# Zero products in three waits of the head, and seven unread transfers taken out

## The chip, the cores and the metric

The kernel runs on one core of a Trainium2 chip. The metric is the device time of one execution in microseconds (us); the time of a kernel is the median of its runs.

## The reference

Two stages, for 4 batches of 12,544 rows of 128 numbers. The first is attention through 32 inducing vectors, the second a maxout layer with two weight matrices:

```python
def mab(q, kv):
    s = scale * (q @ kv.transpose(0, 2, 1))
    s = s - s.max(-1, keepdims=True)
    a = np.exp(s)
    a /= a.sum(-1, keepdims=True) + 1e-09
    return a @ kv
h = mab(I, x)          # I: inducing, 32 x 128, for each of 4 batches
attn = mab(x, h)       # 4 x 12544 x 128
...
h1 = x @ w1            # x: attn as 50176 x 128; w1, w2: 128 x 1024
h2 = x @ w2
g = np.maximum(h1, h2)
return (g @ w_out)     # w_out: 1024 x 128
```

## The kernel before, in words

The maxout is rewritten: max(h1, h2) = h1 + relu(h2 - h1). With w21 = w2 - w1, the first part needs only w1 @ w_out (the tile w1out), and the second a ReLU over the product with w21. As the attention's output is a weighted mean of the 32 rows of h, the product h @ w21 (the tile hwd) is formed once for each batch, and each chunk of 128 rows of x needs only its weights over the 32 rows (the tile e2, exponentials that are divided by their sum at the end).

All engines' orders are written out by hand. The kernel is straight-line code made by a Python program that carries a planner's clock along (class Clock, the object `ck`): `ck.pe`, `ck.act`, `ck.dve`, `ck.pool` and `ck.sp` are the times at which it thinks each engine is free, `ck.bank[i]` the time at which PSUM bank i is free again. `bank()` hands out the bank that comes free first; it marks nothing by itself. `ck.wait(t, why)` moves the planner's PE to t if t is later, `ck.run(us)` adds work to it and a turn between product shapes (`mode`). Real waits are made by semaphores, whatever the planner thinks.

The **head** (batch 0, from L826 on). Nine products of a tile of zeros (`warm`, L831 and L832) run first. x comes in twelve parts. `HEAD` (L858) is a string of words: `1a`, `1b` turn the two halves of a part with PE and copy them out with VectorE and ScalarE (`p1_transpose`, L304); `I` turns the inducing vectors (`head_ind`, L836), whose result `inducingT` VectorE writes at L840; `S0` and so on are a part's scores (`p1_scores`, L323, products at L328); `A0` and so on sum the parts up (`p1_accum`, L352, products at L365 and L374). Then come the small steps: h, its sums (`small_sums`, L543), the first two pieces of hwd (`small_hwd`, L554, product at L569, eviction at L573), the first chunk's exponentials, and one more `fill`, which is so many products of the zeros (L821).

The **stream** follows the string `ORDER` (L1171). `s` is a chunk's exponentials; `p4.9` is a phase (L1099) of up to four units of 32-row products side by side, L1154, each of which a ReLU eviction follows (`relu_out`, L1083: L1091 on VectorE or L1094 on ScalarE, as the bits of the second number say); a bare number is so many products with w_out at L979. The first words are `s p4.9 s p2.2 H1 V W p2.2`. `H1` is the third piece of hwd (step 2 of `small_hwd`: 512 columns, evicted by VectorE), which waits for the last difference w21 that POOL forms at L616. `V` (`weights_2`, L628) turns w1: eight transposes at L634, the second four after POOL's cast at L625; VectorE copies the first four out at L639 and ScalarE the others at L642. `W` (`weights_3`, L647) multiplies that with w_out, eight products at L651, which wait for both copies.

On **SP's queue** the head issues two loads of x and one of the inducing vectors (L277, L278). L291 then issues seven transfers inside the on-chip memory, of 8, 12, 14, 15, 4, 2 and 1 partitions and 16 to 28 bytes each, from the first loaded part of x to a corner of a ReLU buffer (`probe`); nothing reads what they write. They wait for that part. After them SP carries the transposing transfers (L241) and the stores of the output (L1039). The other loads are issued from POOL.

Of the kernel before, what the change touches and what calls it, by code (L numbers as in the profile page):

```python
# [16 lines left out]
INF = 1e9  # L17
# [140 lines left out]
def kernel(  # L158
# [9 lines left out]
    nc = tc.nc  # L168
# [24 lines left out]
    ck = Clock()  # L193
    uid = [0]
    psall = psum.tile([128, 8, 512], F32, name="psall", tag="psall")
    relus = [big.tile([128, 2, 4096], F16, name=f"relus{q}", tag=f"relus{q}") for q in range(4)]
# [3 lines left out]
    def bank(shape, dtype=F32, only=None):  # L200
        i = min(range(8), key=lambda j: ck.bank[j]) if only is None else only
        ps = psall[:, i, :]
        if dtype == F16:
            ps = ps.bitcast(F16)
            if len(shape) == 3:
                ps = ps.rearrange("p (k c) -> p k c", c=128)
            ps = ps[:, 0 : shape[1]]
        return i, ps
# [8 lines left out]
    xn_at = {}  # L217
# [36 lines left out]
    warm = consts.tile([128, 512], F16, name="warm")  # L254
# [7 lines left out]
    w1T = w1s[:, J : 2 * J].rearrange("p (j c) -> p j c", c=C)  # L262
    w21 = consts.tile([C, J], F16, name="w21")
# [2 lines left out]
    inducingT = consts.tile([C, M], F16, name="inducingT")  # L266
    m1bd = consts.tile([128, 4, C], F16, name="m1bd")
    repd = consts.tile([128, 128], F32, name="repd")
    probe = relus[2][0:16, 1, 3968:4096]
    pace = consts.tile([128, 1], F32, name="pace")  # L270

    with tc.manual_schedule(engines={ET.PE, ET.DVE, ET.Activation, ET.Pool, ET.SP}):
# [14 lines left out]
            nc.gpsimd.dma_start(out=w1f[:, sl], in_=moe_w1[:, sl])  # L287
            nc.gpsimd.dma_start(out=w2f[:, sl], in_=moe_w2[:, sl])
        nc.gpsimd.dma_start(out=woutp, in_=moe_w_out.rearrange("(jb j) c -> j jb c", j=128))
        for i, k in enumerate((8, 12, 14, 15, 4, 2, 1)):  # L290
            nc.sync.dma_start(out=probe[0:k, 16 * i : 16 * i + 8 + i], in_=xn_at[0, 1][0:k, 0, 0 : 8 + i])  # L291
        nc.vector.memset(warm, 0.0)
        nc.vector.memset(ones16, 1.0)
        nc.vector.memset(minus1, -1.0)
# [259 lines left out]
        def small_hwd(b, steps=(0, 1), vector=True):  # L554

            if b == 0:
                cuts = ((0, 256), (256, 512), (512, 1024))
            else:
                cuts = ((0, 512), (512, 1024))
            if 0 in steps:  # L560
                st[b]["hwd"] = smp.tile([128, J], F16, name=f"hwd_{b}", tag="hwd")
            hwd = st[b]["hwd"]
            for step in steps:
                lo, hi = cuts[step]
                w, sl = hi - lo, slice(lo, hi)
                bi, ps = bank([128, 512])
                ps = ps[:, 0:w]
                ck.wait(max(ck.bank[bi], st[b]["hT4r"], w_of.get(("w21", lo), 0.0) if b == 0 else 0.0), "p1")
                nc.tensor.matmul(out=ps, lhsT=st[b]["hT4"], rhs=w21[:, sl], start=True, stop=True)  # L569
                end = ck.run(0.215 * w / 512)  # L570
                if b == 0:
                    if vector:
                        nc.vector.tensor_scalar(  # L573
                            out=hwd[:, sl],
                            in0=ps,
                            scalar1=st[0]["rs"],
                            scalar2=1.0 / scale,
                            op0=ALU.mult,
                            op1=ALU.mult,
                        )  # L580
                    else:
                        nc.scalar.activation(out=hwd[:, sl], in_=ps, func=AF.Copy, scale=st[0]["rw"])
                elif step == 0:
                    nc.vector.tensor_copy(out=hwd[:, sl], in_=ps)
                else:
                    nc.scalar.copy(out=hwd[:, sl], in_=ps)
                if vector if b == 0 else step == 0:
                    ck.bank[bi] = ck.on_dve(end, 0.07 + w / 970.0)
                else:
                    ck.bank[bi] = ck.on_act(end, 0.06 + w / 1200.0)  # L590
                for piece in range(lo // 256, hi // 256):
                    st[b]["hw", piece] = ck.bank[bi]
# [19 lines left out]

        w_of = {}

        def difference(eng, lo, hi, ready, us):
            eng.tensor_sub(w21[:, lo:hi], w2f[:, lo:hi], w1f[:, lo:hi])  # L616
            w_of["w21", lo] = ck.on_dve(ready, us) if eng is nc.vector else ck.on_pool(ready, us)

        def cast_w1(h):
            sl = slice(512 * h, 512 * (h + 1))  # L620
            if h == 0:
                nc.vector.tensor_copy(out=w1h[:, sl], in_=w1f[:, sl])
                ck.on_dve(20.4, 0.33)
            else:
                nc.gpsimd.tensor_copy(out=w1h[:, sl], in_=w1f[:, sl])  # L625
                w_of["cast"] = ck.on_pool(0.0, 0.8)
# [19 lines left out]

        def weights_3():  # L647
            bi, ps = bank([128, 512])
            ck.wait(max(ck.bank[bi], w_of["w1T"]), "w")
            for jb in range(NJB):  # L650
                nc.tensor.matmul(  # L651
                    out=ps[:, 0:128],
                    lhsT=w1T[:, jb, :],
                    rhs=woutp[:, jb, :],
                    start=(jb == 0),
                    stop=(jb == NJB - 1),
                )
            end = ck.run(0.056 * NJB)
            nc.scalar.copy(out=w1out, in_=ps[:, 0:128])
            ck.bank[bi] = w_of["w1out"] = ck.on_act(end, 0.2)  # L660
# [158 lines left out]
            ck.bank[bi] = ck.on_dve(end, 0.18 + 0.001 * 4 * n)  # L819

        def fill(n):  # L821
            bi, ps = bank([128, 512])
            for _ in range(n):
                nc.tensor.matmul(out=ps, lhsT=warm[:, 0:128], rhs=warm, start=True, stop=True)
            ck.run(0.22 * n)


        nc.vector.tensor_copy(out=xn_at[0, 0][:, 0:8, :], in_=xf[:, 0:8, :])  # L828
# [1 line left out]
        bi, ps = bank([128, 512])  # L830
# [25 lines left out]
        ck.pe, ck.act = 7.18, 6.25  # L856
        p1_transpose(0, 0, 1)
        HEAD = """  # L858
        1a 1b I S0 2a 2b S1 A0 S2 3a 3b A1 4a 4b S3 S4 A2 A3 5a 5b A4 6a 6b S5 7a 7b S6 A5 8a 8b S7
        A6 9a 9b 10a S8 11a N S9 S10 A7 S11 A8 A9 A10 A11  # L860
        """
        for word in HEAD.split():
            if word == "I":
                head_ind()
            elif word == "N":
                cast_w1(0)
            elif word[0] == "S":
                p1_scores(0, int(word[1:]))
            elif word[0] == "A":
                p1_accum(0, int(word[1:]))  # L870
            else:
                p1_transpose(0, int(word[:-1]), "ab".index(word[-1]))
# [207 lines left out]
            jobs = sorted(jobs, key=lambda e: e[0])[:n]  # L1080
            return gl, [e[1:] for e in sorted(jobs, key=lambda e: e[1])]

        def relu_out(q, blk, unit, bi, ready, vector):  # L1083

            _, t0, w, u = unit
            jpb, w4 = 4 // w, blk.quarters[q].w
            dst = blk.relu[q][:, 0 : NJB * w4 * 128].rearrange("p (j t) -> p j t", j=NJB)
            dst = dst[:, u * jpb : (u + 1) * jpb, 128 * t0 : 128 * (t0 + w)]
            src = psall[:, bi, :].rearrange("p (j t) -> p j t", j=jpb)
            if vector:  # L1090
                nc.vector.tensor_scalar(out=dst, in0=src, scalar1=0.0, scalar2=None, op0=ALU.max)  # L1091
                t = ck.on_dve(ready, 0.604)
            else:
                nc.scalar.activation(out=dst, in_=src, func=AF.Relu)  # L1094
                t = ck.on_act(ready, 0.484)
            ck.bank[bi] = t
            blk.done[q, t0, u] = t

        def phase(n, vector=0):  # L1099
            gl, jobs = pick(n)  # L1100
            free = sorted(range(8), key=lambda j: ck.bank[j])[: len(jobs)]
            got = []
            for (q, blk, unit), bi in zip(jobs, free):
                _, t0, w, u = unit
                pieces = range(u * (4 // w) // 2, ((u + 1) * (4 // w) - 1) // 2 + 1)
                staged = blk.first if blk.first is not None and t0 + w <= 2 else blk.staged
                ready = max([ck.bank[bi], staged] + [st[blk.b]["hw", p] for p in pieces])
# [8 lines left out]
            if gl is not None:  # L1116
                q, b = gl.q, gl.blk.b
# [3 lines left out]
                        out=gl.ps[:, 128 * s : 128 * (s + 1)],  # L1121
                        lhsT=gl.blk.e2[r, 128 * t : 128 * (t + 1)],
# [8 lines left out]
            for q, blk, (_, t0, w, u), bi, ps, ready in got:  # L1131
                r = slice(32 * q, 32 * (q + 1))
                jpb = 4 // w
# [30 lines left out]
            for k, (q, blk, unit, bi, _, _) in enumerate(got):  # L1164
                ready = ends[k] + 0.025
                ptr[q][1] += 1
                state["issued"] += 1
                relu_out(q, blk, unit, bi, ready, bool(vector >> k & 1))

        state["stage"] = 1  # L1170
        ORDER = """  # L1171
# [43 lines left out]
            "p": phase,  # L1215
        }
        for word in ORDER.split():
            if word == "s":
                stage(blocks[state["stage"]])
                state["stage"] += 1  # L1220
            elif word.isdigit() or word[0] == "n":
                narrow = word[0] == "n"
                for _ in range(int(word.lstrip("n"))):
                    ready = final_ready()
                    if not narrow:
                        keep_busy(ready)
                    ck.wait(ready, "relu")
                    final_one(narrow)
            else:
                WORK[word[0]](*[int(n) for n in word[1:].split(".") if n])  # L1230
# [32 lines left out]
```

## Time and profile before

| | us |
|---|---|
| median of 3 runs | 315.84 (315.37, 315.84, 316.93) |
| the profiled execution | 315.13 |
| its span in the trace | 313.3 |
| PE busy in the span | 306.2 (98%) |
| ScalarE (ACT) busy | 280.9 (90%) |
| VectorE (DVE) busy | 273.4 (87%) |
| GpSimd (POOL) busy | 122.4 (39%) |

PE is the matmul engine, PEld its loading of weights, DVE is VectorE, ACT ScalarE, SP the engine whose queue issues most transfers; L569 is line 569 of the kernel. A row of the timeline gives start, length (both us), engine, line and operation, output and inputs, the shapes (for products: rows by columns of the weights, then the moving operand), how many in a row, and in brackets the idle time ahead of them with what ended it. A row of the chain in order of time gives start, length and what the time went to. A row of the waits gives who waited for whom, the total in us, how often, and the longest. Products are pipelined: the length of a row holds the tail of its last product, so the distance between starts says what a product costs.

### The profile page before, as it was taken

What the parts mean: (1) busy time and instruction counts of PE and PEld (TensorE: products, weight loads), DVE (VectorE), ACT (ScalarE), POOL (GpSimd) and SP (SyncE); (2) the same over time, 40 slices, a digit from 0 to 9 for tenths busy, and PEclk for the clock granted to TensorE, in tenths of its full rate; (3) what the DMA queues carried; (4) which work ended last, traced back from release to release, by engine and by line L of the source; (5) the groups of instructions that cost most, each with busy time, mean ns of one, the idle gap of its engine ahead of it and who ended that gap; (6) DMA issues with size and microseconds to landing.
All of it is one profiled execution on the core that took longest, in us unless ns stands there. A gap on an engine that the chain in (4) does not pass through costs nothing.

```text
span 313.3 us, 12580 instructions
## 1 busy us (share of the span) xinstructions
PE 306.2 (98%) x5310; PEld 239.7 (76%) x5310; DVE 273.4 (87%) x485; ACT 280.9 (90%) x581; POOL 122.4 (39%) x183
## 2 busy tenths in 40 slices
PE   8998999999999999999999999999999999999996
PEld 3875777777877777778877887778778877788885
DVE  2468999998889999989899999999999899989894
ACT  3768999999989989999999999989999899998875
POOL 7364008900530006567600563238205742388000
PEclk9999999999999999999999999999999999999999
DMA  7999988999499999997899899993422522352223
GB/s 203 209 260 205 215 223 187 155 235 226 112 205 245 253 208 198 204 185 196 190 239 258 180 228 204 215 200 130 133 86 103 153 101 89 117 130 104 103 88 135
DMA packets 80931, 55.69 MB, mean 178 GB/s; under 512 B 62410, under 2 KB 65770, under 8 KB 80874
## 3 DMA queue, kind: packets, MB, share of 16 engines
q1 hardware_dynamic: 74906, 41.19, 56.7%
q0 software_dynamic: 5968, 13.70, 22.6%
q8 instruction: 41, 0.67, 0.9%
q14 instruction: 16, 0.13, 0.1%
HBM read 27.28 MB, written 25.69 MB: 169 GB/s over the span
## 4 chain that ended last, share of the span: by engine, by line
PE 89%; DMA 6%; ACT 2%; DVE 1%; SPq 1%; issue 1%; POOL 0%; POOLq 0%
PE psall L979 58%; PE psall L1154 21%; DMA xn<-in_x_dram 2%; PE psall L701 2%; DMA xT<-xn 2%; DMA eT<-eu 2%; PE psall L312 1%; PE psall L461 1%; PE psall L402 1%; ACT relus L1094 1%; PE psall L374 1%; PE psall L328 1%; SPq L241 1%; DVE relus L1091 1%; PE psall L569 1%
## 5 line engine op out<-in xcount | busy, mean ns | idle before, releaser
L1094 ACT ACTIVATE relus<-psall 128x512 f16<-128x512 f32 x468 | 239.2, 619 | 15.9 <-PE psall L1154 14.8
L1091 DVE TENSOR_SCALAR relus<-psall 128x512 f16<-128x512 f32 x308 | 195.5, 683 | 16.7 <-PE psall L1154 15.8
L979 PE MATMUL psall<-woutp,relus 128*128 128x128 f16 x3104 | 203.9, 220 | 0.0
L979 PEld LDWEIGHTS <-relus 128*128 128x128 f16 x3104 | 174.9, 98 | 33.5 <-issue 27.7
L1154 PE MATMUL psall<-e,hwd 32*128 32x512 f16 (+2 forms) x840 | 81.1, 362 | 0.0
L765 POOL TENSOR_TENSOR half<-ed 128x256 f32<-128x256 f16 (+2 forms) x22 | 13.4, 611 | 147.0 <-DMA ed<-e 147.0
L769 POOL TENSOR_TENSOR rd<-den,minus 128x16 f32<-128x16 f32 (+2 forms) x22 | 57.8, 2628 | 1.7
L1014 DVE TENSOR_TENSOR osbs<-psall,rd 128x512 f32<-128x512 f32 (+1 forms) x80 | 50.9, 637 | 4.6 <-PE psall L1154 1.6
L1154 PEld LDWEIGHTS <-hwd 32*128 32x128 f16 x880 | 27.8, 91 | 11.6 <-issue 2.3
L1154 PE MATMUL psall<-m,e 32*128 32x128 f16 x372 | 36.6, 216 | 0.0
L1154 PEld LDWEIGHTS <-e 32*128 32x128 f16 x372 | 22.2, 92 | 9.7 <-issue 2.0
L765 POOL TENSOR_TENSOR half<-half 128x32 f32<-128x32 f32 (+4 forms) x66 | 21.4, 324 | 5.2
L228 POOL DMA_DIRECT2D xn<-in_x_dram x32 | 17.6, 562 | 5.6 <-DMA xn<-in_x_dram 4.3
L1014 DVE TENSOR_TENSOR osbs<-psall,rp 128x512 f32<-128x512 f32 (+3 forms) x24 | 15.6, 649 | 0.5 <-PE psall L1154 0.4
L316 DVE COPY xT<-psall 128x512 f16<-128x512 f16 (+3 forms) x12 | 5.7, 485 | 8.5 <-PE psall L312 8.5
L416 ACT ACTIVATE eu<-psall 128x512 f16<-128x512 f32 x18 | 10.8, 611 | 0.3 <-PE psall L402 0.2
L714 ACT ACTIVATE e<-psall 128x512 f16<-128x512 f32 (+2 forms) x21 | 10.9, 574 | 0.1
L319 ACT COPY xT<-psall 128x768 f16<-128x768 f16 (+3 forms) x10 | 5.8, 575 | 4.6 <-PE psall L312 4.5
L701 PE MATMUL psall<-xT,hT 128*32 128x512 f16 (+3 forms) x110 | 8.4, 362 | 0.0
L312 PE MATMUL psall<-identity,xn 128*128 128x128 f16 x98 | 8.0, 229 | 0.4 <-DMA xn<-in_x_dram 0.3
L312 PEld LDWEIGHTS <-xn 128*128 128x128 f16 x98 | 6.1, 103 | 2.3 <-DVE xn L828 1.0
L402 PE MATMUL psall<-xT,inducingT 128*32 128x512 f16 x72 | 6.3, 381 | 0.0
(114 smaller groups left out, 128.2 us busy)
## 6 DMA issues: line engine op xcount, KB each, us to landing
out_dram<-osbs SPq DMA_DIRECT2D x90, 256.0 KB, 2.5
xn<-in_x_dram POOLq DMA_DIRECT2D x24, 448.0 KB, 9.6
out_dram<-osbs SPq DMA_DIRECT2D x10, 128.0 KB, 5.8
relus<-in_moe_w_dram POOLq DMA_DIRECT2D x4, 256.0 KB, 5.8
xn<-in_x_dram POOLq DMA_DIRECT2D x4, 224.0 KB, 10.3
xT<-xn SPq DMA_TRANSPOSE x33, 4.1
relus<-in_x_dram SPq DMA_DIRECT2D x1, 512.0 KB
relus<-in_x_dram SPq DMA_DIRECT2D x1, 384.0 KB
```

The lines of the kernel that those rows point to most:

```text
L228: nc.gpsimd.dma_start(out=xn_at[b, i][:, 0:n, :], in_=xr[b, :, k0 : k0 + n, :])
L312: nc.tensor.transpose(ps[:, j, :], xn[:, g + j, :], identity16)
L416: nc.scalar.activation(out=eu, in_=ps, func=AF.Exp, scale=scale, accum_out=st[b]["es"][:, u : u + 1])
L701: nc.tensor.matmul(out=ps[32 * q : 32 * (q + 1), 128 * t : 128 * (t + n)], lhsT=hq, rhs=xT[:, c : c + n, :], start=True, stop=True, tile_p ...
L714: nc.scalar.activation(out=blk.e2[:, 0 : 128 * wd], in_=ps[:, 0 : 128 * wd], func=AF.Exp, scale=st[0]["rs"] if blk.b == 0 else scale,)
L765: nc.gpsimd.tensor_tensor(out=dst, in0=cur[:, :, 0:n], in1=cur[:, :, n : 2 * n], op=ALU.add)
L769: nc.gpsimd.tensor_tensor(out=rp[:, 0:wd, :].rearrange("p t q -> p (t q)"), in0=den[:, 0 : 4 * wd], in1=minus1[:, 0 : 4 * wd], op=ALU.pow,)
L979: nc.tensor.matmul(out=g.ps[lo:hi, 128 * c : 128 * (c + 1)], lhsT=relu[:, lo:hi], rhs=woutp[:, jb, :], start=not g.started, stop=(state["m ...
L1014: nc.vector.tensor_mul(osb[:, 0:m, :], g.ps[:, 0 : m * C].rearrange("p (s c) -> p s c", s=m), g.blk.rp[:, t0 : t0 + m, q : q + 1].broadcas ...
L1091: nc.vector.tensor_scalar(out=dst, in0=src, scalar1=0.0, scalar2=None, op0=ALU.max)
L1094: nc.scalar.activation(out=dst, in_=src, func=AF.Relu)
L1154: nc.tensor.matmul(**seq.pop(0))
```

## The change

The seven transfers of L291 and their tile are taken out. A function `dummies(ps, n)` issues n products of the tile of zeros into a bank and adds 0.22 us each to the planner's PE. It is called in three places: one product at the new word F of the head's order, between the turned inducing vectors and the first scores; and, ahead of the third piece of batch 0's hwd and ahead of `weights_3`, as many products as the planner's clock has room for, at 0.23 us each, in the bank that the real product then writes. `phase`, `relu_out` and new helpers can also evict two units at once where a word of ORDER has a third number; ORDER itself is unchanged and has no such word.

```diff
-    probe = relus[2][0:16, 1, 3968:4096]
...
-        for i, k in enumerate((8, 12, 14, 15, 4, 2, 1)):
-            nc.sync.dma_start(out=probe[0:k, 16 * i : 16 * i + 8 + i], in_=xn_at[0, 1][0:k, 0, 0 : 8 + i])
...
                 bi, ps = bank([128, 512])
                 ps = ps[:, 0:w]
+                if b == 0 and step == 2:
+                    n = int((w_of["w21", lo] + 0.05 - max(ck.pe, ck.bank[bi])) / 0.23)
+                    if n > 0:
+                        ck.wait(ck.bank[bi], "p1")
+                        dummies(psall[:, bi, :], n)
                 ck.wait(max(ck.bank[bi], st[b]["hT4r"], w_of.get(("w21", lo), 0.0) if b == 0 else 0.0), "p1")
                 nc.tensor.matmul(out=ps, lhsT=st[b]["hT4"], rhs=w21[:, sl], start=True, stop=True)
...
+        def dummies(ps, n):
+            for _ in range(n):
+                nc.tensor.matmul(out=ps, lhsT=warm[:, 0:128], rhs=warm, start=True, stop=True)
+            ck.run(0.22 * n)
+
...
         def weights_3():
             bi, ps = bank([128, 512])
+            n = int((w_of["w1T"] - max(ck.pe, ck.bank[bi])) / 0.23)
+            if n > 0:
+                ck.wait(ck.bank[bi], "w")
+                dummies(ps, n)
             ck.wait(max(ck.bank[bi], w_of["w1T"]), "w")
...
         def fill(n):
-            bi, ps = bank([128, 512])
-            for _ in range(n):
-                nc.tensor.matmul(out=ps, lhsT=warm[:, 0:128], rhs=warm, start=True, stop=True)
-            ck.run(0.22 * n)
+            dummies(bank([128, 512])[1], n)
...
         HEAD = """
-        1a 1b I S0 2a 2b S1 A0 S2 3a 3b A1 4a 4b S3 S4 A2 A3 5a 5b A4 6a 6b S5 7a 7b S6 A5 8a 8b S7
+        1a 1b I F S0 2a 2b S1 A0 S2 3a 3b A1 4a 4b S3 S4 A2 A3 5a 5b A4 6a 6b S5 7a 7b S6 A5 8a 8b S7
...
+            elif word == "F":
+                fill(1)
...
-        def phase(n, vector=0):
+        def phase(n, vector=0, hold=0):
             gl, jobs = pick(n)
-            free = sorted(range(8), key=lambda j: ck.bank[j])[: len(jobs)]
+            taken, pairs, first = {}, set(), {}
...
+                if hold >> k & 1 and q not in taken and follower(blk, q, unit):
...
+            for q, _, _ in jobs:
+                if q not in taken:
+                    taken[q] = min((j for j in range(8) if j not in used), key=lambda j: ck.bank[j])
+                    used.add(taken[q])
+            free = [taken[q] for q, _, _ in jobs]
...
+                else:
+                    relu_out(q, blk, [unit], bi, ready, vector >> k & 1)
```

More of the change, by code (lines that the diff above doesn't have):

```diff
@@ L1081, in pick, with relu_out @@
             return gl, [e[1:] for e in sorted(jobs, key=lambda e: e[1])]
-        def relu_out(q, blk, unit, bi, ready, vector):
-            _, t0, w, u = unit
-            jpb, w4 = 4 // w, blk.quarters[q].w
+        holds = {}
+        def relu_out(q, blk, units, bi, ready, vector):
+            _, t0, w, u = units[0]
+            n, jpb, w4 = len(units), 4 // w, blk.quarters[q].w
             dst = blk.relu[q][:, 0 : NJB * w4 * 128].rearrange("p (j t) -> p j t", j=NJB)
-            dst = dst[:, u * jpb : (u + 1) * jpb, 128 * t0 : 128 * (t0 + w)]
-            src = psall[:, bi, :].rearrange("p (j t) -> p j t", j=jpb)
+            dst = dst[:, u * jpb : (u + n) * jpb, 128 * t0 : 128 * (t0 + w)]
+            if n == 2:
+                src = psall[:, bi : bi + 2, :].rearrange("p v (j t) -> p v j t", j=jpb)
+                dst = dst.rearrange("p (v j) t -> p v j t", v=2)
+            else:
+                src = psall[:, bi, :].rearrange("p (j t) -> p j t", j=jpb)
@@ L1090, in relu_out @@
             if vector:
                 nc.vector.tensor_scalar(out=dst, in0=src, scalar1=0.0, scalar2=None, op0=ALU.max)
-                t = ck.on_dve(ready, 0.604)
+                t = ck.on_dve(ready, (0.604, 1.141)[n - 1])
             else:
                 nc.scalar.activation(out=dst, in_=src, func=AF.Relu)
-                t = ck.on_act(ready, 0.484)
-            ck.bank[bi] = t
-            blk.done[q, t0, u] = t
-        def phase(n, vector=0):
-            gl, jobs = pick(n)
-            free = sorted(range(8), key=lambda j: ck.bank[j])[: len(jobs)]
+                t = ck.on_act(ready, (0.484, 0.915)[n - 1])
@@ new lines, in relu_out, with follower, flush @@
+            for k, (_, t0, _, u) in enumerate(units):
+                ck.bank[bi + k] = t
+                blk.done[q, t0, u] = t
+        def follower(blk, q, unit):
+            k = blk.units[q].index(unit) + 1
+            nxt = blk.units[q][k] if k < len(blk.units[q]) else None
+            return nxt if nxt and nxt[1:3] == unit[1:3] and nxt[3] == unit[3] + 1 else None
+        def flush(keep=()):
+            for q in sorted(holds):
+                if q not in keep:
+                    blk, unit, bi, ready, vector = holds.pop(q)
+                    relu_out(q, blk, [unit], bi, ready, vector)
@@ new lines, in phase @@
+        def phase(n, vector=0, hold=0):
+            gl, jobs = pick(n)
+            taken, pairs, first = {}, set(), {}
+            for q, blk, unit in jobs:
+                if q in holds and holds[q][0] is blk and follower(blk, q, holds[q][1]) == unit:
+                    bi = holds[q][2] + 1
+                    if ck.bank[bi] < INF and bi not in taken.values():
+                        taken[q] = bi
+                        pairs.add(q)
+            flush(pairs)
+            used = set(taken.values())
+            for k, (q, blk, unit) in enumerate(jobs):
+                if hold >> k & 1 and q not in taken and follower(blk, q, unit):
+                    able = [
+                        j for j in range(7)
+                        if not used & {j, j + 1} and max(ck.bank[j], ck.bank[j + 1]) < INF
+                    ]
+                    if able:
+                        taken[q] = min(able, key=lambda j: max(ck.bank[j], ck.bank[j + 1]))
+                        used |= {taken[q], taken[q] + 1}
+                        first[q] = True
+            for q, _, _ in jobs:
[3 more added lines that the diff above has]
+            free = [taken[q] for q, _, _ in jobs]
@@ L1167, in phase @@
                 state["issued"] += 1
-                relu_out(q, blk, unit, bi, ready, bool(vector >> k & 1))
+                if q in pairs:
+                    before = holds.pop(q)
+                    relu_out(q, blk, [before[1], unit], before[2], ready, vector >> k & 1)
+                elif q in first:
+                    holds[q] = (blk, unit, bi, ready, vector >> k & 1)
+                    ck.bank[bi] = INF
+                else:
+                    relu_out(q, blk, [unit], bi, ready, vector >> k & 1)
         state["stage"] = 1
@@ L1217 @@
         for word in ORDER.split():
+            if word[0] != "p":
+                flush()
             if word == "s":
```

## The prediction

> **What bounds the kernel now.** I read the page's busy lines first, then the chain of work that ended last, then the same chain in order of time over the first 50 us, since all three waits of the change lie there.
>
> ```profile
> span 313.3 us, 12580 instructions
> PE 306.2 (98%) x5310; PEld 239.7 (76%) x5310; DVE 273.4 (87%) x485; ACT 280.9 (90%) x581; POOL 122.4 (39%) x183
> PE 89%; DMA 6%; ACT 2%; DVE 1%; SPq 1%; issue 1%; POOL 0%; POOLq 0%
> ```
>
> PE carries 89% of the chain and is busy for 98% of the span. Of 313.3 us at most 313.3 - 306.2 = 7.1 us are idle on PE. What can matter is whether a product is added where PE is on the chain, or where it waits for somebody else.
>
> ```profile
> 2.51 7.31 DMA xn<-in_x_dram
> 9.82 0.05 issue
> 9.87 0.95 PE psall L312 x14
> ...
> 22.97 0.47 PE psall L1154 x4
> 23.44 0.02 issue
> 23.46 1.89 DVE relus L1091 x3
> 25.35 0.66 DVE hwd L573
> 26.01 0.34 DVE relus L639
> 26.35 0.04 issue
> 26.39 0.62 PE psall L651 x8
> ```
>
> In order of time: until 9.82 us the chain is the load of the third part of x, from 9.87 PE's first phase, and from 23.46 to 26.35 it is not PE at all but VectorE: three ReLU evictions, the third piece of hwd, the copy of the turned w1. Then PE takes it up again at L651. So all three places of the change (before 9.21, before 24.32, before 26.39) are stretches in which another resource sets the pace. The waits of PE over the same 50 us say how long each is:
>
> ```profile
> PE psall L651 <- DVE relus L639: 1.1, 1, 1.1
> PE psall L328 <- DVE inducingT L840: 0.4, 1, 0.4
> PE psall L312 <- DMA xn<-in_x_dram: 0.3, 2, 0.2
> PE psall L569 <- POOL w L616: 0.3, 1, 0.3
> ```
>
> **The change, part by part.** *How many products.* One comes from the new word F. For the other two the kernel's planner decides, in whole products of 0.23 us. I carried its arithmetic through the unchanged order: ahead of the third piece of hwd its PE stands at 24.13, the bank's release at 24.02, the difference w21 is due at 24.65, so n = int((24.65 + 0.05 - 24.13) / 0.23) = 2. Ahead of L651 PE stands at 25.67, the bank at 24.97, w1T is due at 26.56, so n = int(0.89 / 0.23) = 3. Six products in all, 5310 + 6 = 5316. Since n is rounded down and charged at 0.22, the planner's PE meets the same due time afterwards; F ends, by its count, at 8.93, ahead of the 9.23 that the scores wait for. So every later bank, job and keep-busy count comes out as before. The new argument hold is 0 in every word of the order, so the pairing of units is never entered, and a single unit's eviction has the old operands.
>
> *What one costs.* The PE rows of the head:
>
> ```profile
> 1.19 4.02 PE L832 MATMUL psall<-warm 128*128 128x512 f16 x9 [1.19 <-DVE ones_q L295]
> 5.27 1.04 PE L312 MATMUL psall<-identity,xn 128*128 128x128 f16 x8
> 6.10 1.06 PE L824 MATMUL psall<-warm 128*128 128x512 f16 x2
> 8.60 0.24 PE L838 MATMUL psall<-relus 32*128 32x32 f32 x1
> 9.21 0.50 PE L328 MATMUL psall<-inducingT,xT 128*128 128x32 f16 x14 [0.37 <-DVE inducingT L840]
> 9.87 0.95 PE L312 MATMUL psall<-identity,xn 128*128 128x128 f16 x14 [0.15 <-DMA xn<-in_x_dram]
> 10.66 0.51 PE L328 MATMUL psall<-inducingT,xT 128*128 128x32 f16 x14
> ```
>
> Read starts, not durations, since products are pipelined. Eight transposes take 6.10 - 5.27 = 0.83 us, 104 ns each; fourteen take 10.66 - 9.87 = 0.79, 56 ns each. So PE begins at half speed, whatever the granted-clock column says there, and is at full speed by 9.87. The nine products of 512 columns cost about 4.02 / 9 = 0.45 us each at half speed. At full speed the nearest row is L569 below, 512 columns wide: 24.53 - 24.32 = 0.21 us. I take 0.21, and 0.45 as the upper bound.
>
> *F.* L838 ends at 8.84, the scores start at 9.21 on VectorE's inducingT: 0.37 us, against 0.21. Even at 0.45 only 0.08 would stick out, and the 0.15 us that PE then waits for the load at 9.87 swallows it. Its bank is the eighth, which nothing has used yet, so it waits for no release. Cost 0.
>
> *The other two.* The rows between 23.4 and 26.4 us:
>
> ```profile
> 23.46 1.89 DVE L1091 TENSOR_SCALAR relus<-psall 128x512 f16<-128x512 f32 x3 [0.46 <-PE psall L1154]
> 23.99 0.10 PEld L569 LDWEIGHTS <-hT 128*128 128x128 f16 x1 [0.21 <-issue]
> 24.20 0.62 POOL L625 CAST relus<-relus 128x512 f16<-128x512 f32 x1
> 24.32 0.38 PE L569 MATMUL psall<-w,hT 128*128 128x512 f16 x1 [0.25 <-POOL w L616]
> 24.53 0.74 PE L634 MATMUL psall<-identity,relus 128*128 128x128 f16 x8
> 25.27 0.74 DVE L573 TENSOR_SCALAR hwd<-psall,rs 128x512 f16<-128x512 f32 x1
> 25.61 0.62 ACT L642 COPY relus<-psall 128x512 f16<-128x512 f16 x1
> 25.93 0.41 DVE L639 COPY relus<-psall 128x512 f16<-128x512 f16 x1
> 26.39 0.62 PE L651 MATMUL psall<-woutp,relus 128*128 128x128 f16 x8 [1.12 <-DVE relus L639]
> 26.95 0.50 PE L1154 MATMUL psall<-e_first,hwd 32*128 32x128 f16 x10
> ```
>
> Ahead of L569 the array takes full-width weights at 23.99 and the product starts at 24.32. Two products fill 23.99 + 0.42 = 24.41: L569 is late by about 0.1 us. Queued behind it on PE are the eight transposes of L634. L569's product is read by L573, which VectorE reaches only at 25.27, 0.57 us after L569's end at 24.70. The transposes end at 25.27, their second half waits for POOL's cast (ends 24.82) anyway, and they are read at 25.61 and 25.93: at least 0.34 us free. And ScalarE's copy, the tighter one, ends at 26.23 while VectorE's ends at 26.34, so 0.34 + 0.11 = 0.45 us may be lost here before L651 moves. Cost 0, covered by VectorE's queue; with that cover gone it would be 0.1.
>
> Ahead of L651 PE is idle for 1.12 us; three products take 0.63 to 1.35 us. The bank there was last read by the second of VectorE's three evictions, which at 1.89 / 3 = 0.63 us each ends near 24.72, before the transposes do, so the products don't wait for it. Cost 0 at full speed; at half speed 0.23. In neither place does an engine other than PE get work.
>
> *The seven transfers.* SP's rows and its queue:
>
> ```profile
> 7.69 5.49 SPq L291 DMA_DIRECT2D relus<-xn  x7
> 30.20 2.52 SPq L1039 DMA_DIRECT2D out_dram<-osbs  x2
> q1 hardware_dynamic: 74906, 41.19, 56.7%
> ```
>
> SP issues them until 13.18 and has nothing else until 30.20, so the 5.49 us of SP's time are worth 0. On the DMA engines they are 8+12+14+15+4+2+1 = 56 short runs. A packet of that queue takes on average 0.567 x 16 x 313.3 / 74906 = 0.038 us; with as many again for the completions, 112 x 0.038 = 4.3 us over 16 engines, 0.27 us each, or 0.53 if one engine has two packets of all seven. That is how much earlier loads behind them can land. But PE's waits above name only two loads, 0.3 us together, at 7.71 and 9.87, and the later one is mostly past before a transfer issued at 7.69 can be in its way. I take 0, bounds -0.3 to 0.
>
> The **sum** is 0, against 315.13 us of the profiled execution (span 313.3 and 1.8 around it). That execution lies 0.71 below the median of the three runs, 315.84. Of the four times seen (315.13, 315.37, 315.84, 316.93) the middle is (315.37 + 315.84) / 2 = 315.6, which is my forecast.
>
> **What the products might buy: PE's speed.** After the longest wait, L651's eight take at most 26.95 - 26.39 = 0.56 us, 70 ns each with the turn to the narrow products in it: full speed, not 104. So in this execution the wait cost no speed and there is nothing to win back. The Trainium skill, "TensorE: Matmul & The Clock Gate", section "What's actually happening", has the same outcome in a rule: the array falls to half clock only after an idle window of about 3.4 us, longer than any wait here; by it the gain is nothing. The same page's "A second HAM failure mode: psum-queue depth-cycling" says otherwise, that short idle times between groups make the clock swing; that would give the first rival, and the 70 ns above speak against it. Its "Part 4: PE-mode transpose" says that transposes don't count as activity; by that the wait would begin at 24.53 and be 1.9 us long, and the head, much of it transposes, should have stayed slow, where the rows show 56 ns at 9.87.
>
> **The rivals.** *The clock falls in some executions* and the products prevent it. For it: the runs lie 316.93 - 315.37 = 1.56 us apart, and PE busy at twice the time per product for some 3 us after 26.39 would cost about half that, 1.5. Against it: 70 ns. The worst runs would go and the median move to the fast ones: (315.13 + 315.37) / 2 = 315.2. Chance 0.15.
>
> *The products stand in the way (slower).* Place: PE's queue ahead of L569. If w21 is ready when the array is, all of the products is delay: 0.42 us at full speed, still under the 0.45 that is free; at half speed 0.90, so 0.90 - 0.45 = 0.45 late at L651, where PE takes the chain up and hands it to the end: 315.6 + 0.45 = 316.0. It decides from 0.45 us of delay, that is from a third product or from half speed. POOL's difference would have to come 0.3 us earlier and PE be slow at 24 us; the rows show neither. Chance 0.05.
>
> *Earlier landings count after all:* 315.6 - 0.3 = 315.3, if a load that PE meets with no room is behind the transfers. Chance 0.05.
>
> *The change doesn't do what it says:* a planner's time moves, and with it banks and fillers of the later order. Sign open, 1 to 2 us either way. Against it: the due times above absorb every product. Chance 0.03.
>
> **How the numbers follow.** No change: 0.72; the four rivals 0.28. A measurement of this kernel can tell about 0.5%, 1.6 us, from no change, and nearly all cases lie inside that. Faster by more needs the first rival in nearly every run or the last one: 0.04. Slower by more needs the second at more than three times its price or the last one: 0.03. Within: 0.93. The range goes from 315.2 less the 0.71 between median and profiled execution, 314.5, to the highest run seen, 316.9.
>
> **What would show it.** Right: 5316 matmuls; the wait ahead of L651 down from 1.12 to about 0.5 us with L651 still within 0.1 of 26.39; L569 near 24.41 and L573 still at 25.27; the scores at 9.21; from 27 us on the same rows in the same order. Wrong: L651 later than 26.5; after a wait, transposes at 104 ns before the change and 56 after it; ReLU evictions or fillers that differ in number; a start at 9.87 that moves by more than 0.1.

## The result, and the profile after

| | before | after |
|---|---|---|
| median, us | 316.08 (315.00 to 317.98, 22 runs) | 315.13 (314.44 to 316.17, 22 runs) |
| ratio of the two, 95% interval | | 0.9965 (0.9949 to 0.9981) |
| profiled execution, us (its span) | 315.13 (313.3) | 315.27 (313.5) |

The changed kernel is 0.35% faster, about 1.1 us by the ratio (the medians differ by 0.95). Yet the two profiled executions are the same to 0.2 us, and it is the kernel before whose execution is the shorter one. What differs is the spread: 11 of before's 22 runs lie above 316.2 us, none of the changed kernel's does. So the gain isn't in the two profiles; it is in executions that neither of them shows.

The waits of PE over the first 50 us of the changed kernel (who waited for whom, the total in us, how often, the longest):

```profile
PE psall L309 <- DMA xn<-in_x_dram: 1.0, 2, 0.8
PE psall L662 <- DVE relus L646: 0.5, 1, 0.5
PE psall L371 <- issue: 0.3, 1, 0.3
```

and its PE rows at the three places of the change:

```profile
8.74 0.39 PE L619 MATMUL psall<-warm 128*128 128x512 f16 x1
9.18 0.50 PE L325 MATMUL psall<-inducingT,xT 128*128 128x32 f16 x14
...
24.03 0.60 PE L619 MATMUL psall<-warm 128*128 128x512 f16 x2
24.47 0.38 PE L571 MATMUL psall<-w,hT 128*128 128x512 f16 x1
24.68 0.64 PE L641 MATMUL psall<-identity,relus 128*128 128x128 f16 x8
25.16 0.81 PE L619 MATMUL psall<-warm 128*128 128x512 f16 x3
26.43 0.62 PE L662 MATMUL psall<-woutp,relus 128*128 128x128 f16 x8 [0.46 <-DVE relus L646]
```

One, two and three products stand where they were expected. The third piece of hwd starts at 24.47 instead of 24.32, VectorE still evicts it at its own time (25.30, before 25.27), and L662, which was L651, starts at 26.43 instead of 26.39. From there the products with w_out stay 0.03 us behind those of before until 70 us. All that was predicted of this execution is there.

### The profile page after: what moved, and what is told of

It is laid out like the page before. It is cut to its first block, busy times and chain, and to the rows that moved or that the text cites. A ratio compares the mean times of both kernels' runs of the same rounds, so it can differ in the third digit from the quotient of the medians.

```text
span 313.5 us, 12570 instructions
## 1 busy us (share of the span) xinstructions
PE 306.4 (98%) x5316; PEld 239.6 (76%) x5316; DVE 273.2 (87%) x485; ACT 280.9 (90%) x581; POOL 122.3 (39%) x183
## 4 chain that ended last, share of the span: by engine, by line
PE 90%; DMA 4%; ACT 2%; SPq 1%; DVE 1%; issue 1%; POOL 0%; POOLq 0%
PE psall L989 59%; PE psall L1205 22%; DMA xn<-in_x_dram 3%; PE psall L712 2%; DMA xT<-xn 2%; PE psall L458 1%; PE psall L399 1%; PE psall L309 1%; ACT relus L1110 1%; SPq L241 1%; PE psall L371 1%; DVE relus L1107 1%; PE psall L325 1%; PE psall L571 1%; ACT eu L413 0%
```

## The experiments

Three theories stood at the start. The prediction's: neither part does anything, and 0.35% is chance. **C**: PE's clock falls, or comes late, in some executions, and the products prevent it. **T**: the transfers cost the time. A fourth, **I**, came up on the way: the transfers hold up the load of PE's own code.

Each kernel ran 12 times beside runs of the kernel before on the same chip. Besides the times, each run has a mean granted clock. PE's half speed for 3.41 us of a span of 313 lowers that mean by 0.0054, so I count a run as *fallen* when its mean is 0.996 or less. A missing record of the clock reads as 1.0 (the profiled execution of the kernel with both products and transfers has none), so some falls can go uncounted.

**The kernel before again.**

> The kernel before once more, unchanged, against itself: how much a ratio of 0.9965 means. All theories: ratio 1.000; its interval says how far two sets of equal kernels fall apart, about 0.002 each way if the runs spread from 315.0 to 318.0 us by chance. If it comes out as far from 1 as 0.0035, the result itself is doubtful.

Measured: 315.93 us, ratio 1.0005 (0.9982 to 1.0028), 314.61 to 317.49, 2 of 12 fallen (both 317.5). So equal kernels agree, and the spread belongs to before. Over all experiments its neighbours were 116 runs of the kernel before: 46 of them fallen, with a mean of 316.99 us, and 70 others with a mean of 315.64. **A fall costs 1.35 us, and 40% of before's runs have one.** Both are rough: 14 of the 70 others lie above 316.3 us, where only 2 of the 87 such runs of the changed kernel and of the kernels with a part of it do, as if some of the 14 had fallen without a record. No trace of the kernel before caught a fall, so its place in that kernel isn't shown directly.

That the clock comes late in the head is no rival: in the thirteen traces that record it full speed begins between 4.00 and 7.16 us, and the two latest belong to short executions, before's own (7.16; 315.13 us) and one of the changed kernel without its last three products (7.12; 314.76 us).

**One part alone: no transfers.** No product added.

```diff
-        for i, k in enumerate((8, 12, 14, 15, 4, 2, 1)):
-            nc.sync.dma_start(out=probe[0:k, 16 * i : 16 * i + 8 + i], in_=xn_at[0, 1][0:k, 0, 0 : 8 + i])
```

> The kernel before with the seven transfers taken out and nothing else. The prediction's theory (the transfers cost nothing): ratio to before 1.000 within 0.0015, and single runs as far apart as before's, up to about 318 us. Rival T (the gain of 0.35% is the transfers'): ratio near 0.9965 and no run above 316.5. Rival C (PE's clock falls or comes late in some executions and the products prevent it): as the first, 1.000 and a wide spread.

Measured: median 314.90, ratio 0.9982 (0.9957 to 1.0006); 3 of 12 fallen (316.13, 316.65, 318.20); the nine others 314.43 to 315.50, mean 314.86. None of the three expectations holds: the falls stay, as without any gain, but the runs without a fall are 0.7 us shorter than before's beside them (mean 315.58). The transfers cost something of their own.

**The other part alone: six products, transfers kept.**

```diff
+                        dummies(psall[:, bi, :], n)
...
+                dummies(ps, n)
...
+        1a 1b I F S0 2a 2b S1 A0 S2 3a 3b A1 4a 4b S3 S4 A2 A3 5a 5b A4 6a 6b S5 7a 7b S6 A5 8a 8b S7
```

> The kernel before with all six products and the seven transfers kept. Rival C: ratio near 0.9965 (0.995 to 0.998), runs between 314.4 and 316.3 us, none near 318. Rival T and the prediction's theory: ratio 1.000 within 0.0015, spread up to 318.

Measured: median 315.37, ratio 0.9975 (0.9958 to 0.9992), 314.85 to 315.98, 1 of 12 fallen. No run is near 318, and the runs without a fall are where before's are (mean 315.43). Together: the products take falls away, and the transfers' removal takes 0.6 to 0.7 us off the rest (314.86 against 315.43 and 315.58).

**Only the three products ahead of weights_3, transfers kept.**

```diff
         def weights_3():
...
+                dummies(ps, n)
```

> The kernel before with the three products ahead of the eight products of weights_3 alone, in the wait of 1.12 us, the longest of the three. Rival C with the clock falling in that wait: most of the gain, ratio 0.9965 to 0.998, no run above 316.5. Rival C with the clock coming late in the head: ratio 1.000 and spread up to 318, since these products come after it. Prediction's theory: 1.000.

Measured: median 315.54, ratio 0.9983 (0.9963 to 1.0003), 314.62 to 316.25, 1 of 12 fallen. No run is above 316.5, as expected of falls that come from that wait. Its profile held something else, at the same place as in the other traces but longer (before's row first):

```profile
16.54 0.24 PE L374 MATMUL psall<-et,xn 128*128 128x32 f16 x3 [0.27 <-issue]
...
17.34 0.24 PE L374 MATMUL psall<-et,xn 128*128 128x32 f16 x3 [1.01 <-issue]
```

In the middle of the fifth sum of the head PE waits 1.01 us for nothing that the profile names; in before it was 0.27.

**A fall made likely: a longer wait.** Transfers out, no products, and

```diff
                 if g == 0:
+                    nc.vector.memset(relus[2][:, 0, 0:1536], 0.0)
                     nc.vector.tensor_copy(out=w1T[:, 0:4, :], in_=ps)
```

> No transfers, no products, and VectorE clears 1536 unused numbers of a ReLU buffer ahead of its copy of the turned w1, so that PE's wait ahead of weights_3 grows by about 0.8 us, from 1.1 to 1.9. Theory C (the share of time that PE is busy in a window decides on the clock, and the window starts anywhere): more runs than before's 11 of 35 have a mean granted clock below 0.996, at least 7 of 12, and these are 1.4 us slower than the others; median 317 us. Rival: the falls have nothing to do with this wait; then the share of such runs stays at about a third or less, all runs are later by the added 0.8 us, median 315.8.

Measured: median 317.09, ratio 1.0033 (1.0005 to 1.0062), 10 of 12 fallen. The fallen lie 2.3 us above the two others (means 317.62 and 315.30), more than the 1.4 expected; three of them have a mean clock of 0.988 or 0.989, as much as two half-speed windows take. And its profile caught a fall. Windows of 3.41 us (length, busy us of PE, PEld, DVE, ACT and POOL with their instructions, then the granted clock PEclk):

```profile
21.86:25.27 3.41, 3.15 (x41) 1.33 (x40) 2.84 (x8) 3.10 (x7) 3.40 (x6) 1.00 1.21 202
25.27:28.69 3.42, 1.55 (x29) 1.16 (x29) 2.20 (x5) 1.75 (x5) 1.66 (x4) 1.00 1.08 210
28.69:32.10 3.41, 3.39 (x32) 2.25 (x30) 2.44 (x7) 2.85 (x7) 0.00 (x0) 0.50 1.05 208
32.10:35.51 3.41, 3.41 (x59) 2.60 (x56) 3.35 (x7) 2.85 (x7) 0.00 (x0) 1.00 1.08 215
```

and the PE rows around it:

```profile
27.14 0.62 PE L649 MATMUL psall<-woutp,relus 128*128 128x128 f16 x8 [1.87 <-DVE relus L637]
27.69 0.50 PE L1152 MATMUL psall<-e_first,hwd 32*128 32x128 f16 x10
...
28.80 1.25 PE L977 MATMUL psall<-woutp,relus 128*128 128x128 f16 x10
29.84 0.31 PE L594 MATMUL psall<-w1out,hT 128*128 128x128 f16 x1
```

The wait ends at 27.14 and the next eight products still run at full speed (27.69 - 27.14 = 0.55, 69 ns each). The clock falls at 28.69, when the window ends: ten products then take 29.84 - 28.80 = 1.04 us, 104 ns each, and one window later the speed is back. Measured against the profile of before, this one is 0.74 us late at 26 us of before's time and 1.97 at 41: the fall itself cost 1.23.

**The same wait, filled.** Transfers out, the six products in, and three more:

```diff
                 ck.wait(ck.bank[bi], "w")
                 dummies(ps, n)
+                for _ in range(3):
+                    nc.tensor.matmul(out=ps, lhsT=warm[:, 0:128], rhs=warm, start=True, stop=True)
```

> The same longer wait with the transfers out, and with the products in: one, two and six instead of three, so that the six (1.3 us) fill most of the 1.9 us ahead of weights_3. Theory C: no run with a mean granted clock below 0.996, median 315.7 to 316.1 us, that is the changed kernel plus the 0.8 us of VectorE's work, and at least 1 us below the kernel with the longer wait alone. Rival (falls independent of the wait): the same share of falls as there.

Measured: median 315.57, 315.19 to 317.00, ratio 0.9983 (0.9961 to 1.0006), none of 12 fallen: 1.5 us under the unfilled wait (a little more than expected), by products of zeros alone. This pair is the direct test of C.

**The transfers twice, products in.**

```diff
-        for i, k in enumerate((8, 12, 14, 15, 4, 2, 1)):
+        for rep in range(2):
+          for i, k in enumerate((8, 12, 14, 15, 4, 2, 1)):
```

> All six products, and the seven transfers issued twice, fourteen in all. Two parts are asked for by now: the products prevent falls of PE's clock, and the transfers cost about 0.3 to 0.5 us of their own. If the transfers cost that: median 315.6 to 316.0 us, at least 0.5 above the changed kernel beside it. If they cost nothing: median within 0.25 us of the changed kernel, and no run with a mean granted clock below 0.996 in either case.

Measured: median 316.06, ratio 0.9993 (0.9970 to 1.0016), 4 of 12 fallen in spite of all six products, which neither side had expected; the others have a median of 315.52. So the transfers cost time, and its profile shows how both effects meet (PE's rows, then the window):

```profile
15.90 0.23 PE L375 MATMUL psall<-et,xn 128*128 128x32 f16 x3
17.35 0.29 PE L375 MATMUL psall<-et,xn 128*128 128x32 f16 x4 [1.23 <-issue]
17.48 0.91 PE L313 MATMUL psall<-identity,xn 128*128 128x128 f16 x7
18.18 0.39 PE L329 MATMUL psall<-inducingT,xT 128*128 128x32 f16 x7
...
13.89:17.30 3.41, 2.23 (x65) 1.97 (x61) 0.63 (x2) 1.65 (x4) 1.08 (x2) 1.00 1.18 204
```

The wait without a name is 1.23 us long here; the window that it lies in ends at 17.30, and behind it seven transposes take 18.18 - 17.48 = 0.70 us, 100 ns each.

**The changed kernel again**, beside the last three.

> The changed kernel once more, beside the others on the same chip. Ratio to before 0.9965 (0.995 to 0.998), median 315.1 to 315.3 us, no run with a mean granted clock below 0.996.

Measured: median 314.95, ratio 0.9964 (0.9944 to 0.9985), a little below the range expected; 2 of 12 fallen (316.18 and 316.60), which was not expected: with the 22 runs of the result, 2 of 34.

**What the nameless wait is.** Between PE's 223rd and 224th product it stands in all fourteen traces, whatever the kernel. With F in, one product more runs ahead of it, and the row splits 3 and 4 instead of 4 and 3: the wait follows the count of instructions, not the place in the work. The trace has the packets of the code queue, 16 KB each. The first one starts at 14.16 to 14.35 us in the kernels without early transfers (13.17 where the count was shifted), and at 13.99, 14.29, 14.49, 14.87 and 15.02 in the five with them; PE goes on 2.2 to 2.5 us after it in each. That gives theory I, and two tests.

*The transfers moved behind it*, by reading the sixth part of x, all six products in:

```diff
-            nc.sync.dma_start(out=probe[0:k, 16 * i : 16 * i + 8 + i], in_=xn_at[0, 1][0:k, 0, 0 : 8 + i])
+            nc.sync.dma_start(out=probe[0:k, 16 * i : 16 * i + 8 + i], in_=xn_at[0, 5][0:k, 0, 0 : 8 + i])
```

> All six products, and the seven transfers read the sixth part of x instead of the second, so that they are issued from about 15.5 us on, behind the load of PE's code that the trace shows at 14.0 to 15.0. Theory I (the early transfers hold up the first 16 KB code packet, so PE runs out of instructions at its 224th product): gap there 0.45 to 0.7 us as in the kernels without transfers, median 314.9 to 315.3 us. Rival (the transfers cost by themselves, wherever they stand): median 315.4 to 316.0, as with the transfers in place.

Measured: median 314.83, ratio 0.9968 (0.9950 to 0.9987), none of 12 fallen. All seven transfers are there, and the head is none the later for them: at 30 us PE is 0.09 us ahead of before's trace. The wait is 0.22 us, shorter than the 0.45 to 0.7 expected:

```profile
16.52 0.27 PE L374 MATMUL psall<-et,xn 128*128 128x32 f16 x4 [0.22 <-issue]
...
140.44 0.40 PE L402 MATMUL psall<-xT,inducingT 128*32 128x512 f16 x3 [0.82 <-DMA xT<-xn]
```

The last row shows that falls aren't the only thing that makes a run late. This profiled execution took 316.43 us at full clock. It falls 1.1 us behind between 135 and 140 us of before's time, where PE waits 0.82 us for a transposing transfer of x. At the same place the trace with the longer wait loses 0.8 us and the one with products and transfers 0.4, the other eleven nothing above 0.03. It comes with transfers and without them; why it comes isn't shown.

*The count shifted*, in the changed kernel:

```diff
-        for _ in range(WARM):
-            nc.tensor.matmul(out=ps, lhsT=warm[:, 0:128], rhs=warm, start=True, stop=True)
+        for _ in range(4 * WARM):
+            nc.tensor.matmul(out=ps[:, 0:128], lhsT=warm[:, 0:128], rhs=warm[:, 0:128], start=True, stop=True)
```

> The changed kernel with 36 products of 128 columns instead of nine of 512 at the start: the same 3.9 us of PE, but 27 products more. Theory I (the stall near 16 us is PE's code running out at a fixed count of instructions): the gap stands again behind PE's 223rd product, which is 27 products earlier in the order, near 15.2 us, in the scores and no longer in the fifth sum; its length 0 to 1 us, so the median is 314.5 to 315.5. Rival (the stall belongs to that place, by a transfer or an eviction it waits for): the gap stays between the same two products of the fifth sum, now the 250th and 251st.

```profile
14.92 0.23 PE L362 MATMUL psall<-ones,et 128*128 128x1 f16 x3
15.51 0.20 PE L362 MATMUL psall<-ones,et 128*96 128x1 f16 x1 [0.36 <-issue]
```

The wait stands behind the 223rd product again, 27 products earlier in the order, in the sums and not in the scores as I had placed it: it follows the count of PE's instructions, as running out of code would. The time was missed: median 316.87, ratio 1.0020 (0.9997 to 1.0044), 7 of 12 fallen. A second wait of this kind, 0.22 us, stood at 20.88, behind the 351st product, 128 after the first, and 2.3 us after the next code packet had started (18.58); the clock fell at 22.21 for two windows on end:

```profile
18.80:22.21 3.41, 2.98 (x70) 2.38 (x68) 2.17 (x9) 1.92 (x8) 2.20 (x5) 1.00 1.26 268
22.21:25.62 3.41, 3.41 (x32) 0.95 (x25) 2.06 (x5) 2.47 (x6) 3.41 (x6) 0.50 1.05 173
25.62:29.04 3.42, 3.42 (x16) 1.76 (x16) 1.94 (x4) 1.68 (x4) 1.59 (x3) 0.50 1.06 205
```

This window, and the one that ended at 17.30 in the kernel with the transfers twice, lie ahead of the products at 24 and 25 us, so those products could add nothing to them.

**Which products matter.** The changed kernel without its three products ahead of weights_3:

```diff
         def weights_3():
...
-                dummies(ps, n)
```

> The changed kernel without its three products ahead of weights_3; the other three stay. Theory C: that wait is where the clock is lost, so about a third of the runs (2 to 6 of 12) have a mean granted clock below 0.996 and lie 1.4 us or more above the others; the others have a median of 314.8 to 315.1 us, as the changed kernel's. Rival (the products at the start of the scores or ahead of the third piece of hwd do it): none or one such run.

Measured: median 314.84, ratio 0.9961 (0.9944 to 0.9979), none of 12 fallen. My expectation fell: the longest wait stays empty (1.1 us in its trace, as before) and nothing is lost. The two products ahead of the third piece of hwd stand within 3 us ahead of that wait's end, so mostly in the same windows. As far as 12 runs can tell, the pair is enough.

**What the clock counts.** Busy time alone it can't be: the window of the kernel without transfers below kept its speed, though PE is busy for less of it than in the one that ended at 22.21 above.

```profile
23.52:26.93 3.41, 2.04 (x25) 1.19 (x23) 2.87 (x5) 2.79 (x6) 3.41 (x6) 1.00 1.06 196
26.93:30.35 3.42, 3.40 (x59) 2.14 (x57) 2.78 (x7) 3.12 (x7) 0.09 (x1) 1.00 1.06 210
```

So I counted, for every window up to 45 us of the traces that record the clock, columns streamed times the share of the 128 x 128 array that each product uses. The three windows at full speed that were followed by a fall have 0.27, 0.30 and 0.34 of the possible, all that kept their speed 0.37 or more. The gap is narrow: a product that crosses the edge of a window can be counted in several ways, which moves single values by up to 0.03. With a limit of 0.36 before's trace has about 20% of the possible window starts with a fall, where 40% of its runs fell, the longer wait's 85 to 90%, the changed kernel's none. The last kernel was the test: the filled longer wait, with its eight products ahead of hwd and weights_3 on a corner of the array.

```diff
-                nc.tensor.matmul(out=ps, lhsT=warm[:, 0:128], rhs=warm, start=True, stop=True)
+                nc.tensor.matmul(out=ps[0:32, :], lhsT=warm[0:32, 0:32], rhs=warm[0:32, :], start=True, stop=True, tile_position=(0, 0))
```

> The longer wait with its eight products, but these use 32 rows and 32 columns of the array instead of 128 and 128: as long in time, one sixteenth of the array. Theory A (the clock goes by the share of the array that works in a window, and is halved below about 0.36): the products add next to nothing, so falls come back as in the longer wait without products, 7 to 11 of 12 runs below 0.996, median 316.9 to 317.7 us. Rival B (it goes by the time that PE is busy, whatever it multiplies): no falls, median 315.4 to 316.0 us as with the full products.

Measured: median 316.01, ratio 0.9985 (0.9963 to 1.0007), 3 of 12 fallen: fewer than theory A's 7, more than theory B's none. A is refuted as it was put: its own count gives a fall to about 65% of the window starts of this kernel's trace, and one window of it that kept its speed has 0.33 to 0.38. B can't be kept either, by the two windows above, though 3 of 12 against none of 12 with the full products can be chance. What exactly is counted stays open. Counting the rows alone (a product of 32 rows as a quarter, whatever its columns) gives about 12% of the starts here, but hardly any (2 to 5%) to the kernel before, 40% of whose runs fell, so it doesn't hold either.

## Why the prediction was right in range and wrong in its cause

*Counts, cover and cost of the products: right.* Two and three besides F; 5316 products; the scores at 9.18, L571 0.15 late against 0.1 forecast, VectorE's eviction and L662 later by 0.03 and 0.04 only. No engine waits for a product of zeros. The slower rival found no ground.

*"In this execution the wait cost no speed and there is nothing to win back": the step that failed.* The sentence holds for the execution that I had, and I carried it to all of them. I had the 1.56 us between before's runs in front of me and put 0.15 on the rival that explains it, whose price of 1.5 us was nearly right. The experiments show that rival at work: 46 of 116 runs of before fall, at 1.35 us, which is 46 / 116 x 1.35 = 0.54 us in the mean; with the products it is 2 of 34. My evidence against it, 70 ns after the wait, couldn't have told: in the longer wait the products right behind the wait run at 69 ns as well, and the fall comes 1.55 us later, at the window's end.

The Trainium skill, "TensorE: Matmul & The Clock Gate", section "What's actually happening", has both halves of this. That the window is free-running, 3413 ns long and unrelated to the kernel's start agrees with the trace: the half speed lasts from 28.69 to 32.10, and where it starts differs from execution to execution. That the clock falls only after an idle window of about 3.4 us, which I set beside the 70 ns as the same outcome, doesn't: PE was busy for 1.55, 2.23 and 2.98 us of the three windows that were followed by a fall.

*"I take 0, bounds -0.3 to 0" for the transfers: the second term that failed, in size and in place.* I looked for their effect on the loads of x and found PE not waiting for them. The experiments put the effect at 0.3 to 0.8 us in the runs without a fall. The means with the transfers in place are 315.64 for before, which may hold uncounted falls, and 315.43 and 315.47 with products added; without them, or with them moved, 314.86, 314.88, 314.93, 315.15, 315.15. The last two kernels of the first group against the second give 0.45.

A part of it is the wait at the 224th product. It is 0.27, 0.25, 0.71 and 1.01 us in the four traces with the seven early transfers, 0.56 in the mean, and 1.23 where they are issued twice; in the eight others that have it at that place it is 0.22 to 0.49, 0.38 in the mean. That is about 0.2 us. The traces agree: at before's 30 us (places counted from the end of the order) these four stand at 0.00, -0.03, 0.20 and 0.85 us against before's trace, 0.26 in the mean, and the five without the early transfers and without added work for VectorE at -0.09 to 0.12, 0.01 in the mean. Where the rest goes stays open.

In two of the five traces the code packet came as early as without the transfers (13.99 and 14.29), one of them the trace that I had, so they make it late often, not always; that they do is the likely reading of few traces, and how is not shown. The row stood in before's waits, and I left it out because the profile names no cause:

```profile
PE psall L374 <- issue: 0.3, 1, 0.3
```

*The planner: right.* Apart from the six, PE's products stand in the two traces in the same order, fillers included; the new eviction code did nothing.

*The sum:* 0 forecast; measured -1.1, of which the falls are about 0.5 and the rest, about 0.6, falls to the transfers by subtraction. The chance of 0.72 was on no change, and the ratio's interval excludes it. That the range held is luck as far as the mechanism goes: it was made from the spread of before's runs, which is as wide as the gain. The rival's 315.2 met the 315.13 partly by luck too, since it left out the transfers.

## What to carry to other kernels

When the runs of a kernel spread further than the effect in question, one profile can't show where the time goes: read the granted clock of every run, and profile again until one with a fall is caught. Short waits that lie close together can cost PE's speed a window later, at a place that shows nothing itself; products of zeros in one of them were enough here, as far as 12 runs of each kind can tell. A transfer that nobody reads need not be free while the engines' code is being loaded: an "issue" wait at a fixed count of instructions is the sign to look for.

## What the runs showed of the hardware that was not expected

- A window of 3.41 us in which PE is busy for 2.98 us can be followed by half speed; a window with 2.04 us need not be.
- Coming back isn't certain after one window: in the kernel with the shifted count, PE was busy throughout the window from 22.21 to 25.62, and the speed stayed at half for a second one.
- PE waits ahead of its 224th product in all fourteen traces, for 0.22 to 1.23 us, until 2.2 to 2.5 us after a 16 KB packet of the code queue has started; in one of them it waits again 128 products later.
